# Two-queue loads, gated weights and zero-padded z views in a cosFormer attention + gated MLP kernel

## The chip, the cores and the metric

The kernel runs on one core of one Trainium2 chip. The metric is the device time of one execution in microseconds; lower is better. Before the change it is 322.19 us, the median of 10 runs (320.26 to 324.1).

## The reference

q, k and v have the shape 8 x 8 x 576 x 64 (batch, heads, sequence, head dimension), float32. The attention is linear: with r = max(x, 0), each of q and k becomes the concatenation of r cos(theta) and r sin(theta), where theta = pi/2 times position/576. The MLP behind it has d_model 512 and d_ff 2048.

```python
kv = einsum('bhsf,bhsd->bhfd', k_p, v)
z = sum(k_p, axis=2)
num = einsum('bhsf,bhfd->bhsd', q_p, kv)
den = einsum('bhsf,bhf->bhs', q_p, z)[..., None] + 1e-06
attn = num / den                       # then heads side by side: x is 4608 x 512
h = x @ w_in
out = (h * (1.0 / (1.0 + exp(-1.702 * h)))) @ w_out
```

## The kernel before, in words

**Stages.** The 4608 tokens are 8 batches of 576 and, for the MLP, 9 blocks of 512. A start-up part does the attention of batch 0. Then stage i (0 to 8) does the MLP of block i, and between its matmuls the attention of batch i + 1. The order of the work is written out by hand: every engine runs its instructions in the order in which the program issues them. Step n of a stage issues for n = 0 to 15 `mm1(i, n)` (four matmuls of 128x512 into an `hps` bank of PSUM, then gelu on ACT), and for n = 16 to 31 four of the sixteen matmuls of an output tile, `mm2`. After step n come the pieces of attention in `work[n]`. In stage 0 the order of `mm2` is part by part over the four tiles t, so that all four tiles end in the last four steps; in later stages it is tile by tile.

**One batch of attention.** `load_part` (L80) brings the first 512 tokens of a tensor (1 MB in lines of 1 KB, called main here) and `load_tail` (L85) the last 64 (128 KB in lines of 256 B). DVE makes relu(q) in two parts (`prep_q`: heads of even and of odd j, each with a main and a tail piece), k (`prep_k`, `prep_k_tail`) and v times cos and v times sin (`prep_v`, five chunks c; chunk 4 is the tail). q is transposed, for batches 0 and 1 by PE (`transpose_pe`), later by DMA, and multiplied with a cos and a sin table into `qT`. `unit_kv` forms kv and, in two more columns, z, for pairs j of heads. z then goes through `mask_z` into `zs`, which has for each of four segments of the sequence a block of 32 weight columns with z in the places of that segment and zeros elsewhere; with these `unit_den` makes all denominators in one PSUM bank, and DVE their reciprocals. `unit_spread` copies them over partitions (PE, then ACT to `invb`), `unit_num` makes the numerators for one half hf of the sequence, and DVE multiplies both into `xT`, the input of `mm1`. Block 1 needs `xT` of both halves of batch 1.

**Stage 0.** `prep_q` of batch 1 stands at step 6, transpose j and its trig product at step 8 + j, `prep_v` of chunk c at 8 + c, `prep_k` at 13 and 14, `unit_kv` at 15, `unit_den` at 18, the spreads at 22 and 28, the numerators at 25 and 31.

**Loads and their gates.** SP issues the loads of q, k and v and the output stores, one queue in order. POOL issues the weight loads, each in four groups, with a cast to bf16. The order between them is kept by small reads: SP reads one element of `w_in_sb` (L426) before it issues batch 1's loads, POOL reads one element of batch 1's v (L428) before it issues w_out, and SP one of `w_out_sb` (L431) before batch 2's loads. In the start-up POOL also does two pieces of elementwise work ahead of the w_in loads (`prep_v(0, 4, 1, PO)` and `prep_k_tail(0, PO)`).

**PSUM and output.** There are two `hps`, two `yps` and four `at` banks. `mm2` writes to `yps`, in stage 0 to `hps` too; ACT copies a finished tile to `ysb` (three buffers), and SP stores it.

Of the kernel before, what the change touches and what calls it, by code (L numbers as in the profile page):

```python
# [12 lines left out]
F32 = mybir.dt.float32  # L13
# [15 lines left out]
def kernel(  # L29
# [33 lines left out]
    def hps_tile():  # L63
        return ps.tile([128, TB], F32, name="hps", bufs=2)

    def yps_tile():
        return ps.tile([128, TB], F32, name="yps", bufs=2)

    def at_tile():
        return ps.tile([128, TB], F32, name="at", bufs=4)  # L70
# [8 lines left out]
    def load_part(t, src, b, h0, h1):  # L79
        nc.sync.dma_start(  # L80
            out=t[:, 256 * h0:256 * h1].rearrange("p (h e) -> p h e", h=h1 - h0),
            in_=src[b, h0:h1, 0:512, :].rearrange("h (p c) d -> p h (c d)", c=4))

    def load_tail(t, src, b):
        nc.sync.dma_start(  # L85
            out=t[0:64, 2048:2560].rearrange("p (h d) -> p h d", h=H),
            in_=src[b, :, 512:576, :].rearrange("h p d -> p h d"))

    def load_new(b):
        for name in ("qf", "vf", "kf"):  # L90
            state[b][name] = two.tile([128, 2560], F32, name=name)

    def load_all(b):
        load_new(b)
        for name, src in (("qf", q), ("vf", v), ("kf", k)):
            load_part(state[b][name], src, b, 0, H)
            load_tail(state[b][name], src, b)

    load_new(0)
    s0 = state[0]  # L100
    load_part(s0["qf"], q, 0, 0, 8)
    load_tail(s0["qf"], q, 0)
    load_part(s0["vf"], v, 0, 0, 8)
    load_tail(s0["vf"], v, 0)
    load_tail(s0["kf"], k, 0)
    load_part(s0["kf"], k, 0, 0, 4)
    load_part(s0["kf"], k, 0, 4, 8)


    tmp = ExitStack()  # L110
# [31 lines left out]
    nc.scalar.activation(trig[:, 1, :], col_f, AF.Sin, scale=scale)  # L142
    gelu0 = const.tile([128, 1], F32)
    nc.scalar.activation(gelu0, halfpi, AF.Gelu_apprx_sigmoid)
    mask_z = const.tile([128, NSEG, 2, NSEG, 4], BF16)
    nc.gpsimd.memset(mask_z, 0.0)
    for hh in range(2):
        for s in range(NSEG):
            nc.gpsimd.memset(mask_z[hh * 64:hh * 64 + 64, s, hh, s, :], 1.0)

    sel_f = tpool.tile([128, NSEG, 2], F32)
    sel_a = tpool.tile([128, NSEG, 2], F32)
# [36 lines left out]
    nc.gpsimd.tensor_tensor(by_row[:, 7:8], by_row[:, 4:5], by_row[:, 5:6], op=ADD)  # L189
    nc.gpsimd.tensor_tensor(by_row[:, 7:8], by_row[:, 7:8], by_row[:, 6:7], op=ADD)  # L190
    nc.gpsimd.tensor_copy(epsm, by_row[0:3, 7:8].to_broadcast([3, SEG]))

    w_in_sb = one.tile([128, NP, d_ff], BF16)
    w_out_sb = one.tile([128, FC, d_model], BF16)
# [31 lines left out]
    def transpose_pe(b, j, step):  # L226
        s = state[b]
        if step == 0:
            s["tp", j] = tp = at_tile().bitcast(BF16)
            for c in range(5):  # L230
                np_ = 128 if c < 4 else 64
                nc.tensor.transpose(tp[:, c * 128:c * 128 + np_],
                                    s["qn"][:np_, c, 2 * j:2 * j + 2, :].rearrange("p h d -> p (h d)"),
                                    ident[:np_, :np_])
            return
        for cs in range(2):
            nc.vector.tensor_tensor(s["qT"][:, j, cs, :], s["tp", j][:, 0:S], trig[:, cs, :], op=MUL)  # L237

    def transpose_dma(b):
        s = state[b]  # L240
# [5 lines left out]

    def prep_trig(b, j):
        s = state[b]
        for cs in range(2):
            nc.vector.tensor_tensor(s["qT"][:, j, cs, :], s["qTr"][:, j, :], trig[:, cs, :], op=MUL)  # L250

    def prep_k(b, h0, h1, on=nc.vector):
        relu(on, kr[:, 0:4, h0 // 2:h1 // 2].rearrange("p c j (hh d) -> p (j hh) c d", hh=2),
             state[b]["kf"][:, 256 * h0:256 * h1].rearrange("p (h c d) -> p h c d", c=4, d=D))
# [19 lines left out]
    def unit_kv(b):  # L274

        s = state[b]
        kv4 = [at_tile()[:, 0:2 * VW].rearrange("p (j e) -> p j e", j=2) for _ in range(2)]
        for j in range(NP):
            for c in range(5):
                for hh in range(2):  # L280
                    w = 64 * (hh ^ (j % 2))
                    nc.tensor.matmul(kv4[j // 2][w:w + 64, j % 2], kr[:, c, j, 64 * hh:64 * hh + 64],  # L282
                                     vt[:, c, 2 * j + hh, :], start=(c == 0), stop=(c == 4))
        s["kvs"], s["zs"] = [], []
        for kv in kv4:
            zs = two.tile([128, 2, 2, NSEG, 32], BF16, name="zs", bufs=2)
            nc.vector.tensor_tensor(  # L287
                zs.rearrange("p j cs s t -> p j cs (s t)"),
                kv[:, :, 128:130].unsqueeze(3).to_broadcast([128, 2, 2, NSEG * 32]),
                mask_z.rearrange("p s hh t r -> p (s hh t r)").unsqueeze(1).unsqueeze(1).to_broadcast(  # L290
                    [128, 2, 2, NSEG * 32]), op=MUL)
            s["zs"] += [zs[:, jj] for jj in range(2)]
        for kv in kv4:
            kvs = two.tile([128, 2, 2, D], BF16, name="kvs", bufs=4)
            kv5 = kv[:, :, 0:128].rearrange("p j (cs e) -> p j cs e", cs=2)
            if b == 0:
                nc.scalar.copy(kvs, kv5)
            else:
                nc.vector.tensor_copy(kvs, kv5)
            s["kvs"] += [kvs[:, jj] for jj in range(2)]  # L300

    def unit_den(b):

        s = state[b]
        den_ps = at_tile()
        nc.tensor.matmul(den_ps[:, 0:SEG], ones[0:3, :], epsm[0:3, :], start=True, stop=False)
        for g in range(NSEG):
            for cs in range(2):
                for j in range(NP):
                    nc.tensor.matmul(den_ps[32 * j:32 * j + 32, 0:SEG], s["zs"][j][:, cs, g, :],  # L310
                                     s["qT"][:, j, cs, ds(g * SEG, SEG)],
                                     start=False, stop=(g == NSEG - 1 and cs == 1))
        inv, pa, pb, comb = [two.tile([128, SEG], dt, name=f"den{n}", bufs=1)
                             for n, dt in enumerate((F32, F32, F32, BF16))]
        nc.vector.reciprocal(inv, den_ps[:, 0:SEG])  # L315
        for o, m in ((pa, 0), (pb, 1)):
            nc.vector.tensor_tensor(o.bitcast(I32), inv.bitcast(I32), bits[:, m:m + 1].to_broadcast([128, SEG]), op=AND)
        nc.vector.tensor_tensor(comb, pa, pb, op=SUB)
        s["comb"] = comb
        s["invb"] = {}  # L320
# [14 lines left out]
            nc.scalar.copy(invb, bps[j][:, 0:HF])  # L335
            s["invb"][j, hf] = invb

    def unit_num(b, hf):

        s = state[b]  # L340
        num_ps = [at_tile() for _ in range(NP)]
        for j2 in range(2):
            for cs in range(2):
                for jj in range(2):
                    j = 2 * j2 + jj
                    for hh in range(2):
                        r, w = 64 * (hh ^ jj), 64 * hh
                        nc.tensor.matmul(num_ps[j][w:w + 64, 0:HF], s["kvs"][j][r:r + 64, cs, :],  # L348
                                         s["qT"][r:r + 64, j, cs, ds(hf * HF, HF)], start=(cs == 0), stop=(cs == 1))
        for j in range(NP):  # L350
            nc.vector.tensor_tensor(xT[:, j, ds(b * S + hf * HF, HF)], num_ps[j][:, 0:HF], s["invb"][j, hf], op=MUL)  # L351


    gT = {}
# [32 lines left out]
    def mm2(i, t, part):  # L387

        if part == 0:
            cur[t] = hps_tile() if i == 0 and t >= 2 else yps_tile()  # L390
        yps = cur[t]
        for fc in range(part * 4, part * 4 + 4):
            nc.tensor.matmul(yps, gT[fc][:, ds(t * 128, 128)], w_out_sb[:, fc, :],  # L393
                             start=(fc == 0), stop=(fc == FC - 1))
        if part == 3:
            ysb = ypool.tile([128, d_model], F32, name="ysb")
            nc.scalar.copy(ysb, yps)  # L397
            for (p0, n, row, step) in pieces(i * 4 + t):
                nc.sync.dma_start(out=out[row:row + (n - 1) * step + 1:step, :], in_=ysb[p0:p0 + n, :])

# [11 lines left out]
    for c in range(5):  # L412
        prep_v(0, c, 0)
    prep_v(0, 3, 1)
    for c in range(3):
        prep_v(0, c, 1, AC)
    prep_v(0, 4, 1, PO)
    prep_k(0, 4, 8)
    prep_k(0, 0, 4, AC)
    prep_k_tail(0, PO)  # L420
    for j in range(2, NP):
        transpose_pe(0, j, 1)

    for g in range(4):
        nc.gpsimd.dma_start(out=w_in_sb[:, :, ts(g, 512)], in_=win_r[:, :, ts(g, 512)])
    nc.sync.dma_start(out=junk[:, 8:9], in_=w_in_sb[0:1, 0, 1022:1024].bitcast(F32))  # L426
    load_all(1)
    nc.gpsimd.tensor_copy(junk[:, 1:2], state[1]["vf"][0:1, 0:1])  # L428
    for g in range(4):
        nc.gpsimd.dma_start(out=w_out_sb[:, ts(g, 4), :], in_=wout_r[:, ts(g, 4), :])  # L430
# [6 lines left out]
    warmup(8)  # L437
    for hf in range(2):
        unit_spread(0, hf)
    for hf in range(2):  # L440
        unit_num(0, hf)
    first = [hps_tile(), hps_tile(), yps_tile(), yps_tile()]
    for kc in range(NP):
        for fc in range(4):
# [83 lines left out]
```

## Time and profile before

| | |
|---|---|
| median of 10 runs | 322.19 us (320.26 to 324.1) |
| the profiled execution | 321.7 us |
| its span | 319.9 us, mean granted TensorE clock 0.993 |
| PE, PEld, DVE, ACT, POOL busy | 302.8, 140.4, 137.4, 136.6, 19.1 us |
| HBM read, written | 36.70 MB, 9.44 MB |
| start of the first mm1 | 25.74 us |
| start of the second mm1 of stage 1 | 68.46 us |

The profile is of one execution. PE is TensorE's matmuls, PEld its weight loads, DVE the vector engine, ACT the scalar engine, POOL GpSimd, and SP the engine that issues most DMAs. The chain of waits follows the work that ended last back through what released each step; a group line gives engine, operation, output and inputs, shapes, count, busy time and mean duration. L with a number is a line of the kernel before. An arrow after an idle time names what ended it. Granted clock is TensorE's, 1.00 being full speed.

### The profile page before, as it was taken

To read this page: it belongs to the slowest core of one execution; us is meant where nothing else is said; L and a number is where in the kernel's file an instruction comes from. 1 tells how busy PE (TensorE), PEld (TensorE's weight loads), DVE (VectorE), ACT (ScalarE), POOL (GpSimd) and SP (SyncE) were. 2 spreads that over 40 slices of the span, in tenths; PEclk is the share of its full clock that TensorE was granted. 3 is DMA by queue.
4 is the path that set the end of the run, shared out by engine and by line. 5 is a ranking of instruction groups with operands and counts; after the bars stand their busy time and mean duration, and the time that the engine had idled before them with its cause. 6 is when DMAs were issued, how large, how long until landed. Compare 5 with 4: busy or idle time off the path is not lost.

```text
span 319.9 us, 5485 instructions
## 1 busy us (share of the span) xinstructions
PE 302.8 (95%) x2173; PEld 140.4 (44%) x2212; DVE 137.4 (43%) x349; ACT 136.6 (43%) x261; POOL 19.1 (6%) x60
## 2 busy tenths in 40 slices
PE   8789969989999999999999999999999999999993
PEld 3344444435444544454445444544454444444441
DVE  3663594185518461855184618641855110000000
ACT  6425420446344634463446344634463446226511
POOL 8740120000000000000000000000000000000000
PEclk9999989999999999999999999999999999999999
DMA  8989999984963496369537953693330220011022
GB/s 197 245 135 267 278 184 204 302 199 107 297 165 84 98 283 189 96 115 297 143 83 112 314 143 96 167 280 110 82 59 0 68 67 2 33 66 33 2 66 66
DMA packets 62189, 45.84 MB, mean 143 GB/s; under 512 B 28884, under 2 KB 57556, under 8 KB 62164
## 3 DMA queue, kind: packets, MB, share of 16 engines
q1 hardware_dynamic: 57940, 41.30, 51.5%
q0 software_dynamic: 4224, 4.19, 8.2%
q8 instruction: 17, 0.28, 0.4%
q14 instruction: 8, 0.07, 0.1%
HBM read 36.70 MB, written 9.44 MB: 144 GB/s over the span
## 4 chain that ended last, share of the span: by engine, by line
PE 81%; DMA 11%; DVE 2%; POOL 1%; issue 1%; SPq 1%; ACT 0%; ACTq 0%
PE yps L393 37%; PE hps L357 34%; DMA vf<-in_v_dram 7%; PE at L282 3%; PE at L348 2%; DMA w_in_sb<-in_moe_w_in_dram 2%; PE hps L393 2%; DMA out_dram<-ysb 2%; PE at L310 1%; DVE vt L271 1%; PE at L330 1%; DVE qT L237 1%; POOL vt L271 1%; POOL kr L209 1%; SPq L80 0%
## 5 line engine op out<-in xcount | busy, mean ns | idle before, releaser
L357 PE MATMUL hps<-xT,w_in_sb 128*128 128x512 bf16 x551 | 126.0, 379 | 2.5 <-ACT ysb L397 1.1
L393 PE MATMUL yps<-w_out_sb,g 128*128 128x512 bf16 x523 | 122.8, 380 | 1.4 <-issue 0.4
L362 ACT ACTIVATE g<-hps 128x512 bf16<-128x512 f32 x142 | 84.9, 598 | 51.4 <-PE hps L357 49.7
L357 PEld LDWEIGHTS <-w_in_sb 128*128 128x128 bf16 x576 | 55.3, 98 | 69.0 <-issue 3.1
L393 PEld LDWEIGHTS <-g 128*128 128x128 bf16 x576 | 53.6, 98 | 65.6 <-issue 3.6
L397 ACT COPY ysb<-yps 128x512 f32<-128x512 f32 x34 | 20.0, 589 | 91.7 <-PE yps L393 69.1
L351 DVE TENSOR_TENSOR xT<-at,invb 128x288 bf16<-128x288 f32 x64 | 24.7, 451 | 69.1 <-PE at L348 69.1
L335 ACT COPY invb<-at 128x288 f32<-128x288 f32 x60 | 19.7, 421 | 23.0 <-PE at L330 23.0
L250 DVE TENSOR_TENSOR qT<-qTr,trig 128x576 bf16<-128x576 bf16 x48 | 18.3, 454 | 22.9 <-DMA qTr<-qn 22.9
L271 DVE TENSOR_SCALAR vt<-vf,cosw 128x512 bf16<-128x512 f32 (+1 forms) x40 | 19.0, 482 | 2.6 <-DMA vf<-in_v_dram 2.6
L209 DVE TENSOR_SCALAR qn<-qf 128x512 bf16<-128x512 f32 (+2 forms) x52 | 14.2, 341 | 10.4 <-DMA qf<-in_q_dram 10.4
L271 DVE TENSOR_SCALAR vt<-vf,sinw 128x512 bf16<-128x512 f32 (+1 forms) x36 | 17.7, 493 | 0.0
L282 PE MATMUL at<-vt,kr 128*64 128x130 bf16 x320 | 12.0, 233 | 5.1 <-DVE kr L209 2.8
L75 PE MATMUL hps<-warm 128*128 128x512 bf16 x52 | 13.7, 419 | 1.2 <-DVE halfpi L114 1.2
L282 PEld LDWEIGHTS <-kr 128*64 128x64 bf16 x320 | 10.3, 117 | 8.9 <-DVE kr L209 3.5
L315 DVE RECIPROCAL den<-at 128x144 f32<-128x144 f32 x8 | 8.5, 1058 | 10.5 <-PE at L310 10.5
L348 PE MATMUL at<-qT,kvs 64*64 64x288 bf16 x256 | 12.2, 289 | 0.4 <-ACT invb L335 0.3
L209 DVE TENSOR_SCALAR kr<-kf 128x1024 bf16<-128x1024 f32 (+1 forms) x22 | 12.1, 600 | 1.1 <-DMA kf<-in_k_dram 1.1
L287 DVE TENSOR_TENSOR zs<-at,mask_z 128x512 bf16<-128x512 f32 x16 | 10.4, 686 | 0.8 <-PE at L282 0.8
L348 PEld LDWEIGHTS <-kvs 64*64 64x64 bf16 x256 | 6.4, 105 | 8.0 <-issue 7.7
L75 PEld LDWEIGHTS <-warm 128*128 128x128 bf16 x52 | 5.1, 105 | 8.0 <-issue 2.4
L393 PE MATMUL hps<-w_out_sb,g 128*128 128x512 bf16 x31 | 7.9, 380 | 0.1
(69 smaller groups left out, 84.6 us busy)
## 6 DMA issues: line engine op xcount, KB each, us to landing
qf<-in_q_dram SPq DMA_DIRECT2D x8, 1024.0 KB, 6.7
vf<-in_v_dram SPq DMA_DIRECT2D x8, 1024.0 KB, 9.1
kf<-in_k_dram SPq DMA_DIRECT2D x7, 1024.0 KB, 10.6
out_dram<-ysb SPq DMA_DIRECT2D x40, 128.0 KB, 2.4
out_dram<-ysb SPq DMA_DIRECT2D x16, 256.0 KB, 2.2
w_in_sb<-in_moe_w_in_dram POOLq DMA_DIRECT2D x4, 512.0 KB, 8.8
w_out_sb<-in_moe_w_out_dram POOLq DMA_DIRECT2D x4, 512.0 KB, 10.3
qf<-in_q_dram SPq DMA_DIRECT2D x8, 128.0 KB, 6.6
```

The source lines that it names most:

```text
L75: nc.tensor.matmul(wps, warm[:, 0:128], warm, start=True, stop=True)
L209: on.tensor_scalar(o, i, 0.0, None, op0=MAX)
L250: nc.vector.tensor_tensor(s["qT"][:, j, cs, :], s["qTr"][:, j, :], trig[:, cs, :], op=MUL)
L271: on.tensor_scalar(o, i, w, None, op0=MUL)
L282: nc.tensor.matmul(kv4[j // 2][w:w + 64, j % 2], kr[:, c, j, 64 * hh:64 * hh + 64], vt[:, c, 2 * j + hh, :], start=(c == 0), stop=(c == 4))
L335: nc.scalar.copy(invb, bps[j][:, 0:HF])
L348: nc.tensor.matmul(num_ps[j][w:w + 64, 0:HF], s["kvs"][j][r:r + 64, cs, :], s["qT"][r:r + 64, j, cs, ds(hf * HF, HF)], start=(cs == 0), st ...
L351: nc.vector.tensor_tensor(xT[:, j, ds(b * S + hf * HF, HF)], num_ps[j][:, 0:HF], s["invb"][j, hf], op=MUL)
L357: nc.tensor.matmul(hps, w_in_sb[:, kc, ds(fc * 128, 128)], xT[:, kc, ds(i * TB, TB)], start=(kc == 0), stop=(kc == NP - 1))
L362: nc.scalar.activation(g, hps, AF.Gelu_apprx_sigmoid)
L393: nc.tensor.matmul(yps, gT[fc][:, ds(t * 128, 128)], w_out_sb[:, fc, :], start=(fc == 0), stop=(fc == FC - 1))
L397: nc.scalar.copy(ysb, yps)
```

## The change

- **Tails on another queue.** Batch 0's three tails are issued on ACT's DMA queue, the mains alone on SP's. For the other batches all six loads stay on SP, the three mains first and the three tails after them.
- **z.** `mask_z` and the masked product go. Two buffers `zbuf` of 48 columns for each j and each of cos and sin are zeroed once by POOL; `unit_kv` copies z into columns 12 to 15 (upper half of the partitions: 28 to 31), and `unit_den` reads for segment g the 32 columns from 12 - 4g on.
- **Trig.** The two products of one j, with cos and with sin, become one instruction with a broadcast input.
- **POOL.** Its two elementwise pieces go to ACT and DVE. Instead it reads one element of batch 0's v and then issues the w_in loads. SP's gate ahead of batch 1's loads reads the third group of w_in instead of the second.
- **Numerators of batch 0.** They go pair of j by pair of j, over both halves each.
- **End of stage 0.** Output tiles 0 and 1 now use `hps`, 2 and 3 `yps`; the copies of tiles 1 and 3 are done by DVE.

```diff
--- before.py
+++ after.py
@@ -81,30 +81,37 @@
             out=t[:, 256 * h0:256 * h1].rearrange("p (h e) -> p h e", h=h1 - h0),
             in_=src[b, h0:h1, 0:512, :].rearrange("h (p c) d -> p h (c d)", c=4))
 
-    def load_tail(t, src, b):
-        nc.sync.dma_start(
+    def load_tail(t, src, b, on):
+        on.dma_start(
             out=t[0:64, 2048:2560].rearrange("p (h d) -> p h d", h=H),
             in_=src[b, :, 512:576, :].rearrange("h p d -> p h d"))
 
+    SRC = (("qf", q), ("vf", v), ("kf", k))
+
     def load_new(b):
-        for name in ("qf", "vf", "kf"):
+        for name, _ in SRC:
             state[b][name] = two.tile([128, 2560], F32, name=name)
+
+    def load_tails(b, on):
+        for name, src in SRC:
+            load_tail(state[b][name], src, b, on)
+
+    def load_mains(b):
+        for name, src in SRC:
+            load_part(state[b][name], src, b, 0, H)
 
     def load_all(b):
         load_new(b)
-        for name, src in (("qf", q), ("vf", v), ("kf", k)):
-            load_part(state[b][name], src, b, 0, H)
-            load_tail(state[b][name], src, b)
+        load_mains(b)
+        load_tails(b, nc.sync)
 
     load_new(0)
     s0 = state[0]
     load_part(s0["qf"], q, 0, 0, 8)
-    load_tail(s0["qf"], q, 0)
     load_part(s0["vf"], v, 0, 0, 8)
-    load_tail(s0["vf"], v, 0)
-    load_tail(s0["kf"], k, 0)
     load_part(s0["kf"], k, 0, 0, 4)
     load_part(s0["kf"], k, 0, 4, 8)
+    load_tails(0, nc.scalar)
 
 
     tmp = ExitStack()
@@ -142,11 +149,6 @@
     nc.scalar.activation(trig[:, 1, :], col_f, AF.Sin, scale=scale)
     gelu0 = const.tile([128, 1], F32)
     nc.scalar.activation(gelu0, halfpi, AF.Gelu_apprx_sigmoid)
-    mask_z = const.tile([128, NSEG, 2, NSEG, 4], BF16)
-    nc.gpsimd.memset(mask_z, 0.0)
-    for hh in range(2):
-        for s in range(NSEG):
-            nc.gpsimd.memset(mask_z[hh * 64:hh * 64 + 64, s, hh, s, :], 1.0)
 
     sel_f = tpool.tile([128, NSEG, 2], F32)
     sel_a = tpool.tile([128, NSEG, 2], F32)
@@ -190,6 +192,12 @@
     nc.gpsimd.tensor_tensor(by_row[:, 7:8], by_row[:, 7:8], by_row[:, 6:7], op=ADD)
     nc.gpsimd.tensor_copy(epsm, by_row[0:3, 7:8].to_broadcast([3, SEG]))
 
+
+
+    zbuf = [one.tile([128, NP, 2, 48], BF16, name=f"zbuf{i}") for i in range(2)]
+    for t in zbuf:
+        nc.gpsimd.memset(t, 0.0)
+
     w_in_sb = one.tile([128, NP, d_ff], BF16)
     w_out_sb = one.tile([128, FC, d_model], BF16)
     win_r = moe_w_in.rearrange("(kc p) f -> p kc f", p=128)
@@ -233,8 +241,7 @@
                                     s["qn"][:np_, c, 2 * j:2 * j + 2, :].rearrange("p h d -> p (h d)"),
                                     ident[:np_, :np_])
             return
-        for cs in range(2):
-            nc.vector.tensor_tensor(s["qT"][:, j, cs, :], s["tp", j][:, 0:S], trig[:, cs, :], op=MUL)
+        nc.vector.tensor_tensor(s["qT"][:, j], s["tp", j][:, 0:S].unsqueeze(1).to_broadcast([128, 2, S]), trig, op=MUL)
 
     def transpose_dma(b):
         s = state[b]
@@ -246,8 +253,7 @@
 
     def prep_trig(b, j):
         s = state[b]
-        for cs in range(2):
-            nc.vector.tensor_tensor(s["qT"][:, j, cs, :], s["qTr"][:, j, :], trig[:, cs, :], op=MUL)
+        nc.vector.tensor_tensor(s["qT"][:, j], s["qTr"][:, j].unsqueeze(1).to_broadcast([128, 2, S]), trig, op=MUL)
 
     def prep_k(b, h0, h1, on=nc.vector):
         relu(on, kr[:, 0:4, h0 // 2:h1 // 2].rearrange("p c j (hh d) -> p (j hh) c d", hh=2),
@@ -281,15 +287,12 @@
                     w = 64 * (hh ^ (j % 2))
                     nc.tensor.matmul(kv4[j // 2][w:w + 64, j % 2], kr[:, c, j, 64 * hh:64 * hh + 64],
                                      vt[:, c, 2 * j + hh, :], start=(c == 0), stop=(c == 4))
-        s["kvs"], s["zs"] = [], []
-        for kv in kv4:
-            zs = two.tile([128, 2, 2, NSEG, 32], BF16, name="zs", bufs=2)
-            nc.vector.tensor_tensor(
-                zs.rearrange("p j cs s t -> p j cs (s t)"),
-                kv[:, :, 128:130].unsqueeze(3).to_broadcast([128, 2, 2, NSEG * 32]),
-                mask_z.rearrange("p s hh t r -> p (s hh t r)").unsqueeze(1).unsqueeze(1).to_broadcast(
-                    [128, 2, 2, NSEG * 32]), op=MUL)
-            s["zs"] += [zs[:, jj] for jj in range(2)]
+        s["kvs"], s["zs"] = [], zbuf[b % 2]
+        for n, kv in enumerate(kv4):
+            for hh in range(2):
+                r = slice(64 * hh, 64 * hh + 64)
+                nc.vector.tensor_copy(s["zs"][r, 2 * n:2 * n + 2, :, ds(12 + 16 * hh, 4)],
+                                      kv[r, :, 128:130].unsqueeze(3).to_broadcast([64, 2, 2, 4]))
         for kv in kv4:
             kvs = two.tile([128, 2, 2, D], BF16, name="kvs", bufs=4)
             kv5 = kv[:, :, 0:128].rearrange("p j (cs e) -> p j cs e", cs=2)
@@ -307,7 +310,7 @@
         for g in range(NSEG):
             for cs in range(2):
                 for j in range(NP):
-                    nc.tensor.matmul(den_ps[32 * j:32 * j + 32, 0:SEG], s["zs"][j][:, cs, g, :],
+                    nc.tensor.matmul(den_ps[32 * j:32 * j + 32, 0:SEG], s["zs"][:, j, cs, ds(12 - 4 * g, 32)],
                                      s["qT"][:, j, cs, ds(g * SEG, SEG)],
                                      start=False, stop=(g == NSEG - 1 and cs == 1))
         inv, pa, pb, comb = [two.tile([128, SEG], dt, name=f"den{n}", bufs=1)
@@ -335,11 +338,11 @@
             nc.scalar.copy(invb, bps[j][:, 0:HF])
             s["invb"][j, hf] = invb
 
-    def unit_num(b, hf):
-
-        s = state[b]
-        num_ps = [at_tile() for _ in range(NP)]
-        for j2 in range(2):
+    def unit_num(b, hf, j2s=(0, 1)):
+
+        s = state[b]
+        num_ps = {j: at_tile() for j2 in j2s for j in (2 * j2, 2 * j2 + 1)}
+        for j2 in j2s:
             for cs in range(2):
                 for jj in range(2):
                     j = 2 * j2 + jj
@@ -347,8 +350,8 @@
                         r, w = 64 * (hh ^ jj), 64 * hh
                         nc.tensor.matmul(num_ps[j][w:w + 64, 0:HF], s["kvs"][j][r:r + 64, cs, :],
                                          s["qT"][r:r + 64, j, cs, ds(hf * HF, HF)], start=(cs == 0), stop=(cs == 1))
-        for j in range(NP):
-            nc.vector.tensor_tensor(xT[:, j, ds(b * S + hf * HF, HF)], num_ps[j][:, 0:HF], s["invb"][j, hf], op=MUL)
+        for j, t in num_ps.items():
+            nc.vector.tensor_tensor(xT[:, j, ds(b * S + hf * HF, HF)], t[:, 0:HF], s["invb"][j, hf], op=MUL)
 
 
     gT = {}
@@ -387,14 +390,17 @@
     def mm2(i, t, part):
 
         if part == 0:
-            cur[t] = hps_tile() if i == 0 and t >= 2 else yps_tile()
+            cur[t] = hps_tile() if i == 0 and t < 2 else yps_tile()
         yps = cur[t]
         for fc in range(part * 4, part * 4 + 4):
             nc.tensor.matmul(yps, gT[fc][:, ds(t * 128, 128)], w_out_sb[:, fc, :],
                              start=(fc == 0), stop=(fc == FC - 1))
         if part == 3:
             ysb = ypool.tile([128, d_model], F32, name="ysb")
-            nc.scalar.copy(ysb, yps)
+            if i == 0 and t % 2:
+                nc.vector.tensor_copy(ysb, yps)
+            else:
+                nc.scalar.copy(ysb, yps)
             for (p0, n, row, step) in pieces(i * 4 + t):
                 nc.sync.dma_start(out=out[row:row + (n - 1) * step + 1:step, :], in_=ysb[p0:p0 + n, :])
 
@@ -412,19 +418,21 @@
     for c in range(5):
         prep_v(0, c, 0)
     prep_v(0, 3, 1)
-    for c in range(3):
+    for c in (0, 1, 2, 4):
         prep_v(0, c, 1, AC)
-    prep_v(0, 4, 1, PO)
+    prep_k_tail(0)
+    prep_k(0, 0, 4, AC)
     prep_k(0, 4, 8)
-    prep_k(0, 0, 4, AC)
-    prep_k_tail(0, PO)
     for j in range(2, NP):
         transpose_pe(0, j, 1)
 
+    nc.gpsimd.tensor_copy(junk[:, 0:1], s0["vf"][0:1, 0:1])
     for g in range(4):
         nc.gpsimd.dma_start(out=w_in_sb[:, :, ts(g, 512)], in_=win_r[:, :, ts(g, 512)])
-    nc.sync.dma_start(out=junk[:, 8:9], in_=w_in_sb[0:1, 0, 1022:1024].bitcast(F32))
-    load_all(1)
+    nc.sync.dma_start(out=junk[:, 8:9], in_=w_in_sb[0:1, 0, 1534:1536].bitcast(F32))
+    load_new(1)
+    load_mains(1)
+    load_tails(1, nc.sync)
     nc.gpsimd.tensor_copy(junk[:, 1:2], state[1]["vf"][0:1, 0:1])
     for g in range(4):
         nc.gpsimd.dma_start(out=w_out_sb[:, ts(g, 4), :], in_=wout_r[:, ts(g, 4), :])
@@ -437,8 +445,9 @@
     warmup(8)
     for hf in range(2):
         unit_spread(0, hf)
-    for hf in range(2):
-        unit_num(0, hf)
+    for j2 in range(2):
+        for hf in range(2):
+            unit_num(0, hf, (j2,))
     first = [hps_tile(), hps_tile(), yps_tile(), yps_tile()]
     for kc in range(NP):
         for fc in range(4):
```

## The prediction

> **What bounds the kernel now.** I read the page first, then the chain of waits in order of time, then the timelines of PE, DVE, ACT and SP up to 70 us, then busy time by two-microsecond windows, then the landings by tile.
>
> ```profile
> PE 302.8 (95%) x2173; PEld 140.4 (44%) x2212; DVE 137.4 (43%) x349; ACT 136.6 (43%) x261; POOL 19.1 (6%) x60
> ...
> PE 81%; DMA 11%; DVE 2%; POOL 1%; issue 1%; SPq 1%; ACT 0%; ACTq 0%
> ```
>
> PE is the bound on average, so the question is where it is not. From the chain:
>
> ```profile
> 12.48 2.11 POOL vt L271
> 14.59 1.62 POOL kr L209
> 16.21 0.96 POOL w_in_sb L425
> 17.17 7.91 DMA w_in_sb<-in_moe_w_in_dram
> ...
> 27.01 11.58 DMA vf<-in_v_dram
> ...
> 45.20 0.61 DVE kr L209
> 45.85 2.38 PE at L282 x40
> ...
> 62.63 5.09 DMA out_dram<-ysb
> 67.82 0.60 ACT ysb L397
> 68.46 0.59 PE hps L357 x2
> ```
>
> From 68.46 to the end the chain is PE almost without a gap (windows of 32 us hold 31.7 us of PE busy time). All that this change can win or lose lies ahead of 68.46. The chain there: two POOL steps hold back POOL's own w_in loads; w_in delays batch 1's loads; these delay DVE's work on batch 1; this delays `unit_kv(1)`; and at the end of stage 0 the fourth `ysb` copy waits for an output DMA, and a stage-1 matmul for that copy. The windows show what the wait at 45 us costs beside its length (columns: length; busy time of PE, PEld, DVE, ACT, POOL with counts; granted clock; DMA share; GB/s):
>
> ```profile
> 26.00:28.00 2.00, 1.95 (x10) 0.94 (x10) 0.79 (x3) 0.00 (x0) 0.00 (x0) 1.00 1.24 206
> 28.00:30.00 2.00, 1.88 (x10) 0.77 (x9) 0.00 (x0) 1.16 (x3) 0.00 (x0) 1.00 1.17 294
> 44.00:46.00 2.00, 0.15 (x4) 0.15 (x6) 2.00 (x6) 0.00 (x0) 0.00 (x0) 0.94 1.08 162
> 46.00:48.00 2.00, 2.00 (x40) 1.99 (x38) 1.43 (x3) 0.00 (x0) 0.00 (x0) 0.50 1.23 204
> ```
>
> After 2.8 us of idle PE the clock fell to 0.50, and 40 matmuls took 2.38 us (1.25 us in every later stage).
>
> **Part by part.** Times are the profiled execution's own: span 319.9 us, run 321.7 us, 0.5 below the median 322.19. A saving in the span is taken off the median one for one.
>
> *Tails of batch 0 on ACT's queue.* Nothing in the trace shows a second queue. SP's three tail issues took 0.77, 2.40 and 1.39 us; ahead of ACT's first table load this is 2.3 to 4.6 us. ACT has 1.45 us idle before qn (7.31) and 2.87 before vt (11.76), so qn on ACT slips by 0.9 to 3.1 us, and the transposes of odd j with it. In the best case the bytes move no later and the mains earlier; in the worst the tails are served last, near 15 us, and q's preparation on DVE ends there, which moves the first mm1 from 25.74 to about 28.5. I take no shift: the mains no longer stand behind tails, and the issue time mostly falls into idle time.
>
> *No POOL work.* vt L271 (2.11) and kr L209 (1.64) go to ACT (0.71 like its other three) and DVE (0.41, the 64x512 row). ACT is free for the first kr half at 14.6, where k landed at 14.5. DVE's ops that ran beside POOL (0.82, 0.83) return to 0.47 and 0.67. Then qT 4 x 0.38 becomes two ops of about 0.70, and two zs of 0.69 become four copies of 16 elements (0.17 to 0.42: the smallest DVE cast and the 256-element kvs cast from PSUM; I take 0.2). `unit_den(0)` starts about 0.7 us earlier. This is covered: mm1 0 to 8 (8.5 us) then ends near 33.5 and the transposes of batch 1 wait anyway. So it counts as nothing, and up to 4 us lost in the start would cost nothing either.
>
> *w_in gated on v.* POOL's new one-element copy waits for v (11.7); behind it on POOL are only the w_in issues, which nobody else waits to pass. They leave at 12 and not 16.17. Batch 0's data runs until about 15.2 (the 14-16 window has share 0.62), and w_in then needs 4 x 0.5 MB at 206 GB/s, 10.2 us: done at 25.4 where it was about 29 (its rate holds through 26-28). The gate on SP moves to the third group, which lands about 2 us before that, so it hides behind w_in's end. Gain for batch 1's loads: 3.5 us; bounds 2.6 (a slow start like that at 18 us) to 4.2 (POOL's whole lead).
>
> The row that speaks against it: w_out was issued beside DVE's prep_v and its first group landed 7.3 us after issue, w_in's 6.4 with DVE less busy; so up to 0.9 us, which w_in hides while k's data runs. The Trainium skill (SBUF — State Buffer, Who interferes with whom) says that DVE copies and tensor_scalar in a two-port mode lock GpSimd out, and with it the writing of its DMA descriptors. By that rule the four issues, now under six such DVE ops, would slip some 2.4 us, and the sum below would shrink to about zero.
>
> *Batch 1: mains, then tails.* q main landed at 25.90 + 8.3 = 34.2; now 30.7. From one tensor to the next takes 4.0 us in batch 2 (v 62.87, k 66.85), 0.85 of it the tail (v tail 0.8 behind v). So v lands at 33.8, k at 37.0, q's tail at 37.8. Here is the cost: `prep_q(1,0)` reads q's tail third, DVE is in order, and behind it stand all trig, prep_v and prep_k ops of batch 1; PE stands at the first transpose from 33.5 to 38, its clock falls as at 45 us, and the mm1 between the transposes run at half speed.
>
> From q's tail DVE needs 1.4 (rest of prep_q) + 4 x 0.70 (trig) + 10 x 0.395 (prep_v) + 1.6 (prep_k) = 9.75, and 0.7 for a trig that waits for a slow transpose (0 to 2.2): kr is done at 48.25, where it was 46.74. kv follows at full clock, 0.7 after, 48.95; it was 48.2, with the clock low for another 1 us. Then 13 mm2 parts (11.2) + den 0.78 + spread 0.24 + num (half 0) 0.61 give the last spread at 61.8; it was 61.91. So the earlier loads only pay for the later tail.
>
> The merged qT op has no row: 576 elements take 0.44. Double without the second fixed part is 0.70; at the rate of zs (1.34 ns an element) it would be 1.5. I take 0.70, as both inner strides stay as they were.
>
> *w_out.* It is issued at v's landing, 34.1 instead of 38.77, and meets the tails. In the trace the q load issued at 25.90 moved nothing while w_in ran, and k landed 10.7 after its issue in clean batch 2, 11.0 with w_out beside it: whoever is ahead is served first, so I charge nothing. The Trainium skill (DMA: Bandwidth & Descriptors, Queues, rings and completion order) says that each engine takes turns between queues, packet by packet. By it q's tail would let a w_out group pass; the first rival prices that from rows.
>
> *End of stage 0.* hps now serves mm2 t = 0, 1, which end first; ysb 1 and 3 go to DVE. Let T be the last spread. ysb 0 is done at T + 0.7, its output lands 2.2 later (the usual; 5.09 here, behind batch 2's loads), ysb 3 takes DVE from T + 3.0 to 3.7. Behind it on DVE wait the four xT products (4 x 0.38), and mm1(1,0) for these: mm1(1,1) starts at T + 5.5. It was T + 6.55. With T = 61.8 this is 67.3 against 68.46. Batch 2's loads, 4 us earlier as w_out is, are done about T + 1, so 2.2 should hold.
>
> *Steady stages.* zs, qT and the later tails have a whole stage of slack (DVE busy 17.2 of 32 us); the den weight loads read shifted 32-column views, 96 ns before, taken as equal; at the 64-column row (109) they would add 0.4 us a batch.
>
> Sum: 67.3 - 68.46 = -1.1 us, all of it from the end of stage 0: 322.19 - 1.1 = 321.1.
>
> **Rivals.** (1) Slower: q's tail is served behind w_out. Each group passing costs 2.55 us on the chain: one gives -1.1 + 2.5 = +1.4, 323.6; two 326. It decides once the tail lands after 40. For it: tails are issued last and w_out earlier; against: the rows above. A merged qT at 1.5 would do the same (+3.2 on the chain); less likely. (2) More gain: the bytes move better without tails between mains, w_in ends a microsecond sooner, the tail lands at 36.5 and PE's stall stays under 2.8 us, without a slow clock: -1.3 - 0.7 more, 319.1; with an unhindered start 318. For it: the gaps in GB/s (135 in slice 3 of the page). (3) It does nothing that counts: tail 0.5 to 1.5 later than I put it, or ysb 3 waits for an output as before: -0.9 to +0.9, 322.
>
> **How the numbers follow.** A measurement of this kernel can tell about 0.3%, 1.0 us. Forecast (320.2 to 321.2) 0.32; more gain 0.20; nothing 0.22; slower 0.26. Faster 0.52, same 0.22, slower 0.26. The range 317.9 to 324.2 takes in one w_out group and the gain case; the forecast's own is 320 to 322.
>
> **What would show it.** Right: w_in issued near 12; the first DVE qn of batch 1 near 31 but its q-tail op near 38; a PE gap of 3 to 4 us near 34 to 38 with the clock at 0.50 after it; kv(1) near 48 at full clock; no ACT wait at ysb, mm1(1,1) near 67. Wrong: q tail after 40, qT ops over 1 us, w_in landing no earlier, xT held on DVE by ysb 3 for more than 1 us, or steady stages longer than 32 us.

## The result and the profile after

The changed kernel takes 323.28 us (median of 13 runs, 322.73 to 324.41) beside 321.69 us for the kernel before (46 runs). The ratio is 1.005 with a 95% interval of 1.0031 to 1.007: slower by 1.6 us, where 1.1 us less was forecast. The profiled execution took 322.83 us with a span of 320.6 us, 0.7 more than the span before.

From here on L with a number is a line of the kernel that the view is of. The page of the changed kernel, engines first and then the queues, shows that little moved in the averages; q10 is ACT's queue with the three tails of batch 0:

```profile
PE 302.7 (94%) x2173; PEld 139.9 (44%) x2212; DVE 132.3 (41%) x336; ACT 135.7 (42%) x260; POOL 16.2 (5%) x52
...
q10 hardware_dynamic: 1584, 0.39, 0.6%
```

The chain of waits of the changed kernel up to 75 us (start, length, what), the stretch that answers to the one shown of before:

```profile
11.45 0.18 POOL junk L429
11.63 1.92 POOL w_in_sb L431 x2
13.54 9.76 DMA w_in_sb<-in_moe_w_in_dram
...
26.58 12.17 DMA qf<-in_q_dram
38.75 0.02 issue
38.77 0.30 DVE qn L217
...
48.60 1.29 PE at L288 x40
...
63.16 0.24 PE at L333 x8
...
67.11 0.46 DVE xT L354
```

The weights are asked for at 11.6 us (16.2 before) and `unit_kv(1)` runs at full clock (1.29 us against 2.38). But what stands in the chain between the two is now q's tail: issued at 26.58, landed at 38.75, with DVE waiting for it. `unit_kv(1)` starts at 48.60; it started at 45.85. DVE's timeline shows the wait by itself, in the brackets at the end of a line. First the kernel before, where the seven pieces of q's preparation ran without a break, then the changed kernel:

```profile
34.26 1.94 DVE L209 TENSOR_SCALAR qn<-qf 128x512 bf16<-128x512 f32 x7 [7.47 <-DMA qf<-in_q_dram]
```

```profile
30.25 0.76 DVE L217 TENSOR_SCALAR qn<-qf 128x512 bf16<-128x512 f32 x2 [5.55 <-DMA qf<-in_q_dram]
38.77 1.23 DVE L217 TENSOR_SCALAR qn<-qf 64x256 bf16<-64x256 f32 x5 [7.77 <-DMA qf<-in_q_dram]
```

The first two pieces, both mains, are done at 31; the other five, two more mains among them, wait 7.77 us, because the next in order is a tail piece. The windows of the changed kernel (columns as before) show what that does to PE:

```profile
34.00:36.00 2.00, 0.00 (x0) 0.00 (x0) 0.00 (x0) 0.00 (x0) 1.93 (x4) 1.00 1.24 255
36.00:38.00 2.00, 0.00 (x0) 0.00 (x0) 0.00 (x0) 0.00 (x0) 1.16 (x2) 0.54 1.42 162
38.00:40.00 2.00, 0.88 (x3) 0.39 (x4) 1.23 (x6) 0.00 (x0) 0.00 (x0) 0.50 1.29 200
40.00:42.00 2.00, 2.00 (x9) 0.90 (x8) 1.66 (x4) 0.60 (x1) 0.00 (x0) 0.50 1.24 207
42.00:44.00 2.00, 2.00 (x10) 0.95 (x10) 1.59 (x4) 0.60 (x1) 0.00 (x0) 0.75 1.24 205
```

PE does nothing from 32.3 to 39.1, and its clock is at half from about 36 to 43. From stage 1 on the kernels run alike: the start of `unit_den` in stages 1, 2, 3 is 83.80, 115.80, 147.79 after and 83.09, 115.09, 147.08 before, a constant 0.71.

### The profile page after: what moved, and what is told of

Same layout as the page of the kernel before. It is cut to its first block, busy times and chain, and to the rows that moved or that the text cites. A ratio compares the mean times of both kernels' runs of the same rounds, so it can differ in the third digit from the quotient of the medians.

```text
span 320.6 us, 5478 instructions
## 1 busy us (share of the span) xinstructions
PE 302.7 (94%) x2173; PEld 139.9 (44%) x2212; DVE 132.3 (41%) x336; ACT 135.7 (42%) x260; POOL 16.2 (5%) x52
## 4 chain that ended last, share of the span: by engine, by line
PE 85%; DMA 10%; SPq 1%; issue 1%; POOL 1%; DVE 0%; ACT 0%; ACTq 0%; DVEq 0%
PE yps L396 37%; PE hps L360 37%; DMA qf<-in_q_dram 4%; DMA vf<-in_v_dram 3%; DMA w_in_sb<-in_moe_w_in_dram 3%; PE at L288 3%; PE at L351 3%; PE hps L396 2%; PE at L313 1%; PE at L333 1%; SPq L80 1%; POOL w_in_sb L431 1%; PE at L240 0%; PE at L309 0%; SPq L432 0%
## 5 line engine op out<-in xcount | busy, mean ns | idle before, releaser
L360 PE MATMUL hps<-xT,w_in_sb 128*128 128x512 bf16 x551 | 127.6, 382 | 2.0 <-DVE xT L354 0.9
L403 ACT COPY ysb<-yps 128x512 f32<-128x512 f32 x33 | 19.3, 586 | 87.3 <-PE yps L396 65.1
L256 DVE TENSOR_TENSOR qT<-qTr,trig 128x1152 bf16<-128x1152 bf16 x24 | 16.6, 754 | 22.9 <-DMA qTr<-qn 22.9
L288 PE MATMUL at<-vt,kr 128*64 128x130 bf16 x320 | 10.6, 221 | 1.1 <-ACT kr L215 1.1
L288 PEld LDWEIGHTS <-kr 128*64 128x64 bf16 x320 | 9.3, 109 | 4.6 <-issue 2.5
L240 PE MATMUL at<-ident,qn 128*128 128x128 bf16 (+1 forms) x40 | 4.4, 227 | 6.8 <-DVE qn L217 6.8
```

What stands on the lines that cost most here:

```text
L256: nc.vector.tensor_tensor(s["qT"][:, j], s["qTr"][:, j].unsqueeze(1).to_broadcast([128, 2, S]), trig, op=MUL)
L360: nc.tensor.matmul(hps, w_in_sb[:, kc, ds(fc * 128, 128)], xT[:, kc, ds(i * TB, TB)], start=(kc == 0), stop=(kc == NP - 1))
```

## Experiments

Theory A: two large terms of opposite sign. The early w_in is a real gain; mains ahead of tails for batch 1 is a larger loss. Rival B: w_out, issued earlier too, delays the tails. Rival C: the cost lies in the new end of stage 0 or in the start-up. Theory A2, on the new end, and theory D, on the length of the steady stages, are stated with the runs that test them; T is the start of the last spread of stage 0, as in the prediction. A span is that of the one profiled execution of a run.

### The old order of batch 1's loads (e1_order)

```diff
-    load_mains(1)
-    load_tails(1, nc.sync)
+    for name, src in SRC:
+        load_part(state[1][name], src, 1, 0, H)
+        load_tail(state[1][name], src, 1, nc.sync)
```

> The changed kernel, but batch 1's loads keep the order of before (q main, q tail, v main, v tail, k main, k tail). Theory A (q's tail behind three mains eats what the earlier loads bring): q's tail lands near 31 instead of 38.8, PE has no gap at 34 to 38 and no slow clock, kv(1) ends near 42.6 instead of 49.9, the last spread T is near 56 instead of 63.1. But batch 2's loads still end near 64, so the first output of stage 0 lands late, the fourth ysb copy holds DVE and the xT products until then, and the span only falls to about 319.4 (1.2 below the changed kernel, 0.5 below before). If instead the order is harmless (rival B: w_out's traffic delays the tail), the tail still lands after 36 and kv(1) ends after 48.

Measured: ratio 1.0022 (0.9991 to 1.0053), span 320.1. DVE's q pieces ran from 30.72 without a break, PE had no gap at 34 to 38, T fell from 63.10 to 58.73. Almost all of it was given back at the end of stage 0. The chain of this run:

```profile
58.83 0.02 ACT ysb L403
...
59.44 4.81 DMA out_dram<-ysb
...
64.38 0.06 DVE ysb L401
...
64.99 0.46 DVE xT L354
...
65.49 2.12 PE hps L360 x6
```

The first output is issued at 59.44, but batch 2's loads stand ahead of it on SP's queue; it lands at 64.3, and only then can the fourth `ysb` copy, on DVE, go, and the xT products behind it. PE idles 3.14 us ahead of stage 1, and its clock falls to 0.50 (window 68 to 70). So the order is what costs at `unit_kv(1)`, and the end of the stage hides how much. The span was 0.7 above what was expected, and T 2.7: `unit_kv(1)` ended at 44.5 and not at 42.6, and the clock was low behind it too, down to 0.50 in the window 44 to 46.

### w_out only after batch 1's last tail (e2_wout_late)

```diff
-    nc.gpsimd.tensor_copy(junk[:, 1:2], state[1]["vf"][0:1, 0:1])
+    nc.gpsimd.tensor_copy(junk[:, 1:2], state[1]["kf"][0:1, 2048:2049])
```

> The changed kernel, but POOL waits for batch 1's k tail and not its v main before it issues w_out. Rival B (w_out gets ahead of the tails): q's tail lands by 37 instead of 38.77. Theory A (the tail is late because of its place in SP's queue): it lands at 38.5 to 38.8 as before. The time itself says nothing on this, because batch 2's loads start some 6 us later and the outputs of stage 0 queue behind them: 323 to 326 in both.

Measured, in two executions: ratio 1.0112 (1.0042 to 1.0182), span 321.8. w_out was issued at 39.8 and not at 34.2, and q's tail piece on DVE started at 38.71 (38.77 in the changed kernel). The loads were issued 0.84 us later here, so a fair measure is from the first q piece to the tail piece: 8.19 us against 8.52. Rival B explains 0.3 us by that measure, 0.9 at most if the later issue is counted in full, not the 7.8 that DVE waits.

### The old end of stage 0 (e3_old_end)

```diff
-            cur[t] = hps_tile() if i == 0 and t < 2 else yps_tile()
+            cur[t] = hps_tile() if i == 0 and t >= 2 else yps_tile()
...
-            if i == 0 and t % 2:
-                nc.vector.tensor_copy(ysb, yps)
-            else:
-                nc.scalar.copy(ysb, yps)
+            nc.scalar.copy(ysb, yps)
```

> The changed kernel with the end of stage 0 of before (tiles 2 and 3 in hps, all four ysb copies on ACT). If the new end brings what the prediction put on it (1.05 us), the span grows by about 1 us to 321.6. Theory A2 (the new end moves the wait for the output DMA from ACT to DVE, in front of the xT products, and brings nothing once the output lands in 2.5 us): xT starts 0.4 us earlier at 66.7, and the second mm1 of stage 1 at 68.5 instead of 69.05: the span falls by about 0.5 us to 320.1.

Measured: ratio 1.0051 (1.0026 to 1.0075), span 321.1: no difference from the changed kernel. Stage 1's first mm1 started 3.99 us after T (64.33 and 68.32), against 4.51 in the changed kernel (63.10 and 67.61), the half microsecond of theory A2. But T itself was 1.2 later: q's tail landed 0.5 later, and the slow clock lasted to about 45 us in this run and not to 43. The local reading speaks for A2; by the time the two ends are equal here, and neither expectation of the span can be called met.

### Mains first in the kernel before (e4_before_mains)

```diff
-    load_all(1)
+    load_new(1)
+    for name, src in (("qf", q), ("vf", v), ("kf", k)):
+        load_part(state[1][name], src, 1, 0, H)
+    for name, src in (("qf", q), ("vf", v), ("kf", k)):
+        load_tail(state[1][name], src, 1)
```

> The kernel before with one part of the change alone: batch 1's loads as three mains, then three tails. Theory A: q's tail lands near 42.7 (34.2 + 2 x 3.85 + 0.85) instead of 35, kr is done near 53 instead of 46.7, T is near 67 instead of 61.9; the fourth ysb copy then no longer waits for an output, and the span grows by about 4 us to 324. If the order is harmless: no change, 320.

Measured: ratio 1.0105 (1.006 to 1.015), span 324.9. The chain of this run:

```profile
30.96 12.54 DMA qf<-in_q_dram
43.50 0.02 issue
43.53 0.30 DVE qn L209
...
53.58 1.42 PE at L282 x40
...
68.28 0.24 PE at L330 x8
```

The order alone costs 1.05%, some 3.4 us: this part is the loss, in a kernel without any other part of the change. The tail came 0.8 later and T 1.3 later than expected. The profiled execution was the longest of the six; the ratio goes by all of them.

### No wait at the end of stage 0 (e5_order_y4, e6_order_oldend_y4, e11_y4)

e5 is e1 with a fourth `ysb` buffer, e6 the same with the old end, e11, added after e5 and e6 had shown longer steady stages, the changed kernel with the fourth buffer alone. Theory D says that the fourth buffer itself lengthens these stages.

```diff
-    ypool = ctx.enter_context(tc.tile_pool(name="ypool", bufs=3))
+    ypool = ctx.enter_context(tc.tile_pool(name="ypool", bufs=4))
```

> The changed kernel with batch 1's loads in the old order (as in e1_order) and a fourth ysb buffer, so that no copy of stage 0 waits for an output DMA. Theory A says that the 7 us which the early w_in and the old order bring at kv(1) were swallowed by the wait for the first output (3.1 us of idle PE at 62 to 65 in e1_order, and a slow clock after it): T stays near 58.7, xT follows at 62.3, the second mm1 of stage 1 starts near 64.2, and the span falls to about 315.8, 4 us below before. If batch 2's loads, which end near 64, are the real limit, stage 1 waits for them and the span stays near 319.

> As e5_order_y4, but with the old end of stage 0 (tiles 2 and 3 in hps, copies on ACT). Theory A2 (a ysb copy on DVE in front of the xT products costs about 0.5 us, nothing else differs once no copy waits): 0.5 us below e5_order_y4, a span of about 315.3. If the new end is worth its 1.05 us, it is a microsecond above e5_order_y4.

> The changed kernel with a fourth ysb buffer and nothing else. The fourth copy waits no longer for the first output (0.4 us in the changed kernel), so stage 1 starts up to 0.4 us earlier. Theory D: the stages become 32.25 us, so that the span grows by about 1.6 to 322. Otherwise: 320.2, stages of 32.0.

Measured: e5 0.9933 (0.9906 to 0.9961), span 316.7; e6 0.994 (0.9913 to 0.9966), span 316.3; e11 1.0111 (1.0078 to 1.0145), span 321.4. In e5 and e6 stage 1's first mm1 starts at 61.99 and 61.62; batch 2's loads are no limit. Stage 1 thus starts 5.6 to 6.0 us earlier than in the changed kernel, but the span is only 3.9 to 4.3 shorter: the steady stages are 32.25 us long (`unit_den` at 110.43, 142.67, 174.92 in e5). e11 has stages of 32.25 too, so the buffer does it; its profiled execution was the shortest of nine, and the median is 325.35 us. The old end is worth 0.16 us after T here (3.99 in e6 against 4.15 in e5), not 0.5; the medians (319.36 in e6, 319.06 in e5) don't tell the two apart.

### The early w_in alone, in the kernel before (e7_before_early_w)

```diff
-    prep_v(0, 4, 1, PO)
+    prep_v(0, 4, 1, AC)
...
-    prep_k_tail(0, PO)
+    prep_k_tail(0)
...
+    nc.gpsimd.tensor_copy(junk[:, 0:1], s0["vf"][0:1, 0:1])
...
-    nc.sync.dma_start(out=junk[:, 8:9], in_=w_in_sb[0:1, 0, 1022:1024].bitcast(F32))
+    nc.sync.dma_start(out=junk[:, 8:9], in_=w_in_sb[0:1, 0, 1534:1536].bitcast(F32))
```

> The kernel before with one part of the change alone: no elementwise work on POOL, w_in gated on v, and SP's gate on the third group of w_in. Loads in the old order, old end, three ysb buffers. Theory A: q's tail lands near 31, kv(1) ends near 45, T is near 59; the fourth ysb copy on ACT waits for the first output until about 64.4, but the xT products do not, so the second mm1 of stage 1 starts near 65 and the span falls by 3.4 us to 316.5. If the early loads are worth nothing by themselves, the span stays near 320.

Measured: ratio 0.9944 (0.9915 to 0.9973), span 317.4. The chain of this run:

```profile
10.96 1.83 POOL w_in_sb L426 x2
12.80 10.80 DMA w_in_sb<-in_moe_w_in_dram
...
25.53 10.42 DMA vf<-in_v_dram
...
58.84 5.85 DMA out_dram<-ysb
64.79 0.59 ACT ysb L397
65.42 9.66 PE hps L357 x44
```

w_in brings 0.56%, 1.8 us; its span was 0.9 above what was expected. The last three lines show what still swallows the rest: the first output takes 5.85 us to land, the fourth copy waits 3.78 us for it on ACT, and PE 1.84 us for that copy.

e7 against e1 shows more. Both have the early w_in and the old order, but e7's ratio lies below e1's, 0.9944 (0.9915 to 0.9973) against 1.0022 (0.9991 to 1.0053), some 2.5 us (the median spans are 317.5 and 319.8). In both the fourth copy starts when the first output has landed, at 64.79 and 64.38. With the old end (e7) DVE has by then made `xT` (61.60), stage 1 has begun (62.11), and its clock stays at 1.00 in the windows from 62 to 72; with the new end (e1) the copy stands on DVE ahead of these products and stage 1 begins at 65.49. So the new end, no loss beside late tails (e3), is one as soon as the loads come early. The two runs also differ in the z views, the merged products, the second queue and the order of batch 0's work, which e9 and e10 below show to be worth little.

### Batch 0's tails back on SP (e8_tails_sp)

```diff
     load_part(s0["qf"], q, 0, 0, 8)
+    load_tail(s0["qf"], q, 0, nc.sync)
     load_part(s0["vf"], v, 0, 0, 8)
+    load_tail(s0["vf"], v, 0, nc.sync)
+    load_tail(s0["kf"], k, 0, nc.sync)
     load_part(s0["kf"], k, 0, 0, 4)
     load_part(s0["kf"], k, 0, 4, 8)
-    load_tails(0, nc.scalar)
```

> The changed kernel with batch 0's tails back on SP in the order of before. By the prediction the start-up counts as nothing as long as w_in is not late: q's tail of batch 1 lands within 0.7 us of 38.77, and the span is within 0.7 us of the changed kernel's 320.6. If ACT's queue helps (mains no longer behind tails), w_in and all behind it come up to 1 us later and the span grows by as much.

Measured: ratio 1.0056 (1.0031 to 1.0081), the same as the changed kernel's 1.005; span 319.7, 0.9 below it in one execution and so 0.2 outside what was expected, with PE's wait for the q tail ending at 38.64 (39.12). Over all executions the median spans are 321.15 and 321.1. The second queue is neither gain nor loss that these runs can tell.

### The fourth copy in a used-up buffer (e9_order_oldend_dead, e10_early_w_dead)

e9 is the changed kernel with old order and old end, e10 is e7; in both:

```diff
-            ysb = ypool.tile([128, d_model], F32, name="ysb")
+            if i == 0 and t == 3:
+                ysb = state[1]["qf"][:, 0:d_model]
+            else:
+                ysb = ypool.tile([128, d_model], F32, name="ysb")
```

> The changed kernel with batch 1's loads in the old order and the old end of stage 0; the fourth ysb copy of stage 0 goes into batch 1's q buffer, whose data is used up by then, and not into a fourth ysb buffer. Theory D (the fourth ysb buffer itself made each steady stage 0.25 us longer, 32.25 instead of 32.0 in e5 and e6; the waits of stage 0 are the rest): stages of 32.0, second mm1 of stage 1 near 62.6 as in e6, a span of 314.3, 2 us below e6 and 5.6 below before. If the early start of stage 1 itself lengthens the stages (more traffic beside them), they stay at 32.25 and the span at 316.3.

> The kernel before with the early w_in alone (as e7_before_early_w) and the fourth copy of stage 0 in batch 1's used-up q buffer. Theory A with the end of stage 0 freed: the 1.84 us wait of mm1 for the fourth copy in e7 goes, second mm1 of stage 1 near 63, a span of about 315, 2.4 below e7. Stages of 32.0.

Measured: e9 0.988 (0.9835 to 0.9926), median 317.9, span 316.1; e10 0.9878 (0.9829 to 0.9927), median 317.33, span 316.2. Both beat the kernel before and the changed one. One steady window of e5, then the same of e9:

```profile
112.00:144.00 32.00, 32.00 (x250) 14.61 (x248) 16.17 (x43) 14.41 (x28) 0.00 (x0) 1.00 0.66 166
```

```profile
112.00:144.00 32.00, 31.73 (x245) 14.77 (x249) 16.50 (x43) 14.41 (x28) 0.00 (x0) 1.00 0.66 170
```

In e9 the stages are 32.0 us again (`unit_den` at 111.33, 143.32, 175.32), which with e11 settles theory D: it is the fourth buffer that lengthens the stages, not the early start. Its span is 1.8 above what was expected, mostly because stage 1 began 1.5 later than in e6 (63.14): T was 59.15 and not 57.63, after a slow clock at 44 to 48. e10's span is 1.2 above what was expected. Its chain ends stage 0 without a wait:

```profile
58.91 0.24 PE at L330 x8
...
62.32 0.47 DVE xT L351
62.79 0.05 issue
62.84 1.90 PE hps L357 x6
```

## Why the prediction was wrong

The mechanism was the right one and the sign was not. The forecast set an earlier w_in against a later q tail, and got 0 for the two together and -1.1 for the end of the stage. In the spans it was 1.8 us off (+0.7 and not -1.1). By its steps:

- *w_in gated on v.* Issue at 11.6 (12 was said), q main at 30.25 (30.7). Right, and worth 1.8 us by itself (e7). The gate was not quite hidden: between w_in's end and the first of q's data the DMA share fell to 0.50 and 91 GB/s in the window 24 to 26, where it was 1.24 and 207 before. The slowing of the issue that the Trainium skill (SBUF — State Buffer, Who interferes with whom) foresees may be there in part: the four issues took 4.02 us beside DVE's work on v against 3.24; no run separates the two. But w_in's first group landed 6.0 us after issue (6.4 before), so the 2.4 us put on that rule did not appear.
- *The step that failed: "0.85 of it the tail".* A main without a tail behind it was to take 3.15 us; it took 3.8 (q, v, k mains at 30.25, 34.07, 37.9). The other runs with the changed kernel's mains first agree: from q's main to k's it is 7.4 to 7.7 us (e2, e3, e8, e11), where 6.3 was said. q's tail landed at 38.75 and not at 37.8. That is 0.95 of the 1.8 us.
- *DVE's chain from the tail.* 9.75 + 0.7 was said; 38.77 to 49.07 is 10.3. Right, the merged qT at 0.75 and the two waits for slow transposes (0.34, 0.41) included.
- *From kv(1) to T.* 12.85 was said; 49.89 to 63.10 is 13.2: the other 0.35.
- *The end of stage 0.* The output landed in 2.5 us, but was issued at T + 0.7 and reached DVE as T + 3.4, not T + 3.0, and stage 1's second mm1 came near T + 5.95, not T + 5.5 (gelu of the first starts at 69.11): the last 0.45. The forecast put the whole gain here, on the new end. But with the old end (e3) that mm1 comes near T + 5.5 too (gelu of the first at 69.82, T 64.33): the gain on the kernel before is that batch 2's loads are out of the way, and the new end takes some of it back, 0.2 to 0.5 us (e3, e5 and e6) and far more when the output is late (e1 against e7).
- *"A saving in the span is taken off the median one for one."* Not so. A run's time less its span is 1.73 to 1.85 us in every execution on record of the kernel before, e4, e7 and e10, and 2.08 to 2.32 in every execution of the changed kernel and the eight runs built on it. So the change also adds 0.4 us outside the span, which the forecast put at nothing. e8 has it without the second queue, e9 with the old order and the old end; what is left, the z views, the merged products and the order of batch 0's work, was not tested part by part.
- *The start-up counts as nothing.* Right: the first mm1 came at 23.66, 2.1 earlier than before, and PE then waited longer.
- *w_out beside the tails.* "Whoever is ahead is served first": held to 0.3 us (0.9 at most, e2). The alternation of queues of the Trainium skill (DMA: Bandwidth & Descriptors, Queues, rings and completion order) did not cost a w_out group of 2.55 us here.

Of the rivals it was the third, with the first half of its condition, the tail 0.95 later than put; the spans (+0.7) lie in its range, the medians (+1.6) above it. The slower kernel did not come from the first one: the tail landed before 40.

The 1.6 us between the medians are these 0.7, the 0.4 outside the span, and 0.5 because the profiled execution was one of the shorter ones (its span 320.6, the median of the 13 spans 321.1; the profiled execution of the kernel before, 321.7 us, is at its median). The parts taken singly agree with the medians: early w_in -0.56% (e7), mains first +1.05% (e4), together +0.49%, and +0.5% was measured; with half-widths of 0.29 and 0.45 points that agreement is closer than the runs can vouch for, and by e1 (+0.22% with the order kept, not -0.56%) the parts of the change don't simply add. The z views, the merged products, the second queue, the order of the numerators have no share that the ratios can tell, beyond the 0.4 us: e9 has them all and e10 none, and their ratios are 0.988 and 0.9878, each known to about 0.45 points.

What the forecast should have asked was why the sum of a 3.5 us gain and a reordering came to nothing: with the order kept, the loads' gain would have stood out (T at 58.73 in e1), and with it the wait for the first output that then becomes the limit.

## What to carry to other kernels

A load that is needed first belongs first in its queue, all of it: if an in-order engine reads a small piece of tensor 1 early, the large loads put ahead of that piece cost it their whole time (q's tail landed at 31.2 in e1 and at 38.75 behind v and k). Gain and loss in one change can each be larger than the net, here 1.8 and 3.4 us for a net of 1.6; price them apart, and test them apart. After a wait has been shortened, look for the buffer that is next in line: here an output store behind prefetch loads on one queue held a copy, and the copy the next stage, until a fourth place to write was found.

## What the runs showed of the hardware that was not expected

- **The length of PE's pause alone does not decide whether the clock falls.** PE idle for 2.46 us ahead of `unit_kv(1)` kept its clock in e5 (1.00 in every window from 40 to 46), while 2.38 us in e9 was followed by 0.54 and 0.61 (44 to 48), and 1.90 us in e1 by 0.78, 0.50 and 0.86 (42 to 48). The runs don't show what decides. In and after the long gap of the changed kernel the clock was low for some 6.8 us, twice as long as in the kernel before.
- **A buffer more can slow the steady stages.** With four `ysb` buffers in place of three, every steady stage took 32.25 us and not 32.0 (e5, e6, e11). In e5 the chain through them names PE alone: from the sixteenth mm1 matmul of a stage on, every eighth started 0.26 us after the one ahead and not 0.22. The runs don't show why; that the place of the other tiles in memory moves with it was not tested.
- **A small piece put last waits for all that is ahead of it.** With the early w_in, from q's main to k's took 7.4 to 7.7 us without tails in between (the changed kernel, e2, e3, e8, e11) and 7.6 to 8.4 with two (e1, e5, e6, e7, e9, e10): on the mean a tail in between cost the tensor behind it some 0.3 us. At the end the three tails landed 0.7 to 1.0 us apart (38.75, 39.77, 40.5 in the changed kernel), and the first of them waited for both other mains.
